# Loads, weight conversions, merges and the last stores rearranged in a Fourier mixing and gated feed-forward kernel

## The chip, the cores and the metric

The kernel runs on one core of one Trainium2 chip. The time is device time of one execution in microseconds (us); several executions are taken, and their median counts. Engines: PE does the matmuls (PEld its weight loads), DVE and POOL work elementwise on SBUF, ACT evaluates functions and copies, SP only issues transfers. DVE and ACT also read PSUM, where matmuls write. Every engine runs its own instructions in program order; semaphores order the engines among each other.

## The reference

Two stages with one tensor between them. The shapes are batch 8, sequence 3008, width 256, hidden width 1536.

```python
X = np.fft.fft(x, axis=1)
X = np.fft.fft(X, axis=2)
x = X.real.astype(np.float32).reshape(8 * 3008, 256)
gate = 1.0 / (1.0 + np.exp(-(x @ w_gate)))
val = x @ w_val
out = (gate * val @ w_out).astype(np.float32)
```

x is float32. The three weight matrices arrive as float64 and are read as pairs of 32-bit words.

## The kernel before

**Mixing.** The real part of a 2-D transform is a cosine sum minus a sine sum. Rows s, S-s, M+s and M-s of the sequence are loaded together (`x4`, 126 partitions x 4 x 6 x 256), and `fold_ops` adds and subtracts them: `point` (L222) adds a row to its mirror, `first` (L225) does column 0, the unnamed pair at L237 and L238 adds and subtracts the two halves, and `feat` (L228 to L230) folds the features. The sums over the sequence are matmuls with a cosine and a sine table `st` (`half`, groups of an even and an odd PSUM bank, `ev` and `od`); ACT copies `ev` to `a` (L276), and DVE adds and subtracts it with `od` (`places`, L280 and L283) into `pk` (cosine), `qk` (sine) and `ek` (the middle feature). The transform over features isn't done on the data: it is merged into the weights, `merge` (L188) multiplies the table `dt` with a block of gate or value weights, and ACT copies the result to `G1` and `G2`; two small transfers then bring one row of `G2` to `ge` (L198).

**Feed-forward.** For each batch, 6 chunks of sequence positions (five of 256, the last 225) and 6 pairs of hidden blocks, two steps per pair. A step is: `front`, four products `pa` and `pb` on PE and `ae`, `z`, `z` on DVE (L343, L346, L347); `gate` of the step before, `h` on DVE (L358) and one or three sums `sf` on POOL; `back` of the pair two before, 3 or 4 products into the PSUM banks `po0` to `po3`; then the sigmoid on ACT (L543), one entry of the list `later` and the entries of `side`. After a chunk's last pair `finish` copies the banks to `c7` (ACT, L399), adds the slots (POOL, on DVE for the last chunk), transposes 32x32 blocks into `os` (DVE, L406) and stores them with SP, four transfers for each of two halves of the output rows, and four more for rows beyond the last full block of 32.

**Weights.** There are 18 jobs: gate, value and output blocks in turn (0 and 1: gate and value of block 0; 2, 3, 4: gate and value of block 1, output of block 0; and so on). A job is: a load of 512 KB on SP; `weight_parts`, two instructions of ACT; `weight_join`, three of DVE (L174, L175, L177) and one add of POOL (L179), which together turn float64 into float32; then `weight_use`, that is `merge` for gate and value, and `forms` for the output weights (two copies on ACT, four subtractions on POOL). The raw words of jobs 0 to 4 lie in the three places of the tile `z`; those of later jobs lie in `mega`, which takes the space of batch 0's `x4`, and a job's load there waits for the add of the job three before.

**Order.** It is written out by hand and nothing is rearranged. In the opening, loads are issued (x and cosine table in thirds, weights 0 and 1, sine table in thirds, weights 2 to 4); three folds and the cosine products follow, then conversions 0 and 1 between the evacuations, the sine products with merges 0 and 1 between them (L467 to L471), conversions 2 to 4 and the sines' evacuation. Within a step, `pre` is run before the sigmoid (conversions of later weights on ACT), `side` after it (their joins, the loads three jobs ahead, and the uses). Block c of the weights is first needed in step 2c.

```python
    for i in range(2 * len(pairs)):
        done, fresh = fresh, front(i // 2, i % 2)
        if done is not None:
            gate(*done)
        if i >= 4:
            back(i // 2 - 2, i % 2)
        for f in pre.pop(i, []):
            f()
        z = fresh[2]
        nc.scalar.activation(z[:, 0], z[:, 0], AF.Sigmoid)
        if later:
            later.pop(0)()
        for f in side.pop(i, []):
            f()
```

PSUM banks of the opening and of `pa`, `pb` and the merges come from one ring of four (`psx`).

Of the kernel before, what the change touches and what calls it, by code (L numbers as in the profile page):

```python
# [45 lines left out]
def kernel(  # L46
# [56 lines left out]
    def rows(out, src):  # L103

        m = NP // 16 * 16
        nc.sync.dma_start(out=out[0:m], in_=src[0:m])
        nc.sync.dma_start(out=out[m:NP], in_=src[m:NP])

    def load_x(b, nq):
        X[b] = xp.tile([NP, 4, NQ, D], F32, name="x4", tag="x4")  # L110
        return [lambda q=q: rows(X[b][:, :, q : q + nq], xf[b, :, :, q : q + nq])
                for q in range(0, NQ, nq)]
# [11 lines left out]
    def load_table(t, nq):  # L124
        return [lambda q=q: rows(st[:, t, q : q + nq], stab[:, t, q : q + nq])
                for q in range(0, NQ, nq)]
# [7 lines left out]
    KEEP = 5  # L134

    def weight_load(j):

        w, c = jobs[j]
        src = (moe_w_gate, moe_w_val, moe_w_out)[w]
        src = src[2 * c * P : 2 * (c + 1) * P, :] if w == 2 else src[:, c * WC : (c + 1) * WC]  # L140
        src = src.rearrange("(c p) f -> p c f", p=P)
        if j < KEEP:
            raw = zp.tile([P, 2, WC, 2], I32, name="raw", tag="z")
            ws = (app if j < 3 else hp).tile([P, 2, WC], F32, name="ws", tag="ae" if j < 3 else "h")
        else:
            if not mega:
                mega.append(xp.tile([P, 12, 2 * WC], F32, name="mega", tag="x4"))
            r, i = (j - KEEP) % 3 * 2, 6 + (j - KEEP) % 6
            raw = mega[0][:, r : r + 2].rearrange("p a n -> p (a n)").bitcast(I32).rearrange(
                "p (c f w) -> p c f w", c=2, w=2)  # L150
            ws = mega[0][:, i].rearrange("p (c f) -> p c f", c=2)
        WS[j] = ws
        if src.dtype == F32:
            nc.sync.dma_start(out=ws, in_=src)
        else:
            RAW[j] = raw
            nc.sync.dma_start(out=raw.rearrange("p c f w -> p c (f w)"), in_=src.bitcast(I32))
# [58 lines left out]
    def fold_ops(b, eng, nq):  # L216
        x4 = X.pop(b)
        tt = eng.tensor_tensor
        ops = []

        def point(i, j, q):
            tt(x4[:, i, q, 1:D], x4[:, i, q, 1:D], x4[:, j, q, D - 1 : 0 : -1], op=ALU.add)  # L222

        def first(i, j, q):
            tt(x4[:, i, q, 0], x4[:, i, q, 0], x4[:, j, q, 0], op=ALU.add)  # L225

        def feat(v, r, q):
            eng.memset(r[:, q, 0:1], 0.0)  # L228
            tt(r[:, q, 1:HD], v[:, q, 1:HD], v[:, q, D - 1 : HD : -1], op=ALU.subtract)  # L229
            tt(v[:, q, 1:HD], v[:, q, 1:HD], v[:, q, D - 1 : HD : -1], op=ALU.add)  # L230

        parts = [(x4[:, 1 + 2 * blk], x4[:, 2 * blk]) for blk in range(2)]
        qs = [slice(q, q + nq) for q in range(0, NQ, nq)]

        def kind(q):
            two = [[lambda i=i: point(i, i + 1, q)] for i in (0, 2)]
            return two + [[lambda: tt(x4[:, 1, q], x4[:, 0, q], x4[:, 2, q], op=ALU.add)],  # L237
                          [lambda: tt(x4[:, 3, q], x4[:, 0, q], x4[:, 2, q], op=ALU.subtract)]] + [  # L238
                [lambda v=v, r=r: feat(v, r, q)] for v, r in parts]

        if b:

            for n, group in enumerate(zip(*[kind(q) for q in qs])):
                ops += [f for fs in group for f in fs]
                if n < 2:
                    ops.append(lambda n=n: first(2 * n, 2 * n + 1, slice(0, NQ)))
        else:

            for q in qs:
                part = []  # L250
                for n, fs in enumerate(kind(q)):
                    part += fs
                    if n < 2:
                        part.append(lambda n=n, q=q: first(2 * n, 2 * n + 1, q))
                ops.append(lambda part=part: [f() for f in part])
        for blk, (v, r) in enumerate(parts):
            W[b, blk] = (v[:, :, 0:HD], r[:, :, 0:HD],
                         v[:, :, HD : HD + 1].to_broadcast([NP, NQ, P]))
        return ops
# [113 lines left out]
    def back(p, part):  # L373
        b, c, i = pairs[p]
        n = chunks[c][1]
        if part == 0 and i == 0:
            PO[:] = [pso.tile([P, 2, CH], F32, name=f"po{t}", tag=f"po{t}") for t in range(4)]
        h, s = H[p], SF[p]
        move = {1: h[:, 0, 0], 2: h[:, 1, 0], 3: s[:, 3], 4: h[:, 1, 1], 5: s[:, 0], 6: s[:, 1],
                7: s[:, 2]}  # L380
        for m in ORDER[part]:
            t, j = SLOT[m]
            mm(PO[t][:, j, 0:n], wf[:, i, m - 1], move[m], i == 0 and m in FIRST,
               i == NPR - 1)
        if part == 0 and i == NPR - 1:
            PO.append(cp.tile([P, 7, CH], F32, name="c7", tag="c7"))
            nc.scalar.copy(PO[4][:, 6, 0:n], PO[3][:, 0, 0:n])
        if part:
            del H[p], SF[p]
            if i == NPR - 1:  # L390
                finish(b, c, nc.vector if p == len(pairs) - 1 else nc.gpsimd)

    def finish(b, c, eng):
        k0, n = chunks[c]
        nb = -(-n // TB)
        t = PO[4]
        os_ = op.tile([P, 2, CH // TB, 2, TB], F32, name="os", tag="os")
        for j in (0, 2, 1):
            nc.scalar.copy(t[:, 2 * j : 2 * j + 2, 0:n], PO[j][:, :, 0:n])  # L399
# [3 lines left out]
        tt = eng.tensor_tensor  # L403
# [4 lines left out]
        def store(s):  # L408
# [3 lines left out]
            full = m // TB  # L412
            for a in range(4):
                ps = slice(a * TB, (a + 1) * TB)
                cs = slice(a * 2 * TB, (a + 1) * 2 * TB)
                nc.sync.dma_start(
# [6 lines left out]

        later.extend([
# [23 lines left out]
    for j in range(2, KEEP):  # L448
        weight_load(j)
    seq_start(0)  # L450
    folds0 = fold_ops(0, nc.vector, 2)
    cos = [seq_group(0, blk, what, (2 * blk, 2 * blk + 1) if what else None)
           for what in (0, 2) for blk in range(2)]
    for i, f in enumerate(folds0):
# [7 lines left out]
    cos[1][1]()()  # L462
    weight_join(1)
    for _, then in cos[2:]:
        then()()
# [6 lines left out]
    for j in range(2, KEEP):  # L472
        weight_parts(j)
    for _, then in sin:
        then()()
    for j in range(2, KEEP):
        weight_join(j)
# [13 lines left out]
    def weight_step(i, *js):  # L491

        for j in js:
            pre.setdefault(i, []).append(lambda j=j: weight_parts(j))
            at(i, lambda j=j: weight_join(j))
            if j + 3 < len(jobs):
# [3 lines left out]
    for c in range(1, NPR):  # L500
        i = 2 * (c - 1)
        j = 3 * c - 1
        at(i, lambda j=j: weight_use(j))
        at(i + 1, lambda j=j: weight_use(j + 1))
        at(i + (c > 1), lambda j=j: weight_use(j + 2))
        if c + 1 < NPR:
            weight_step(i, j + 3)
            weight_step(i + 1, j + 4, j + 5)
        else:
            weight_step(i, j + 3)  # L510
            at(i + 1, lambda j=j: weight_use(j + 3))
# [3 lines left out]
    for b in range(B - 1):  # L515
# [5 lines left out]
        def folds(f0=f0, b=b):  # L521
            for j, f in enumerate(fold_ops(b + 1, nc.gpsimd, 2)):
# [83 lines left out]
```

## Time and profile before

| | |
|---|---|
| Median of 9 runs | 2045.38 us (2044.51 to 2048.5) |
| Profiled execution | 2045.07 us, span of its records 2043.1 us |
| PE busy | 2003.1 us (98%), 9168 matmul passes |
| DVE busy | 1752.0 us (86%), 3239 instructions |
| POOL busy | 1323.5 us (65%) |
| ACT busy | 500.4 us (24%) |
| Granted TensorE clock, mean | 0.993 |
| HBM traffic | 44.50 MB read, 24.68 MB written |

Parts of the span, from the timeline: loads, folds and the first sums up to about 44 us; the first `pa` at 47.4 us; conversions and merges of weights beside steps 0 to 9, up to about 113 us; after that PE without a pause until its last pass ends at 2033.4 us; sums, transposes and stores of the last chunk until 2043.1 us. The chain of waits that ended last lies on PE for 84% of the span, on DVE for 8% and on POOL for 4%.

How to read the lines: the page gives busy tenths in 40 slices of the span (some 51 us each), with the clock that was granted to PE in tenths. A timeline line has start, duration, engine, source line, operation, tile written <- tiles read, shape, how many instructions were merged into the line, and in brackets the idle time before it with what ended it. Lines of the windows give start:end, length, busy time and number of instructions of each engine, the granted clock, the busy share of the DMA engines, and GB/s. A line of waits gives who waited for whom, the sum, how often, and the longest. "SPq" and "ACTq" are the issues of transfers on those engines' queues.

### The profile page before, as it was taken

What the parts mean: (1) busy time and instruction counts of PE and PEld (TensorE: products, weight loads), DVE (VectorE), ACT (ScalarE), POOL (GpSimd) and SP (SyncE); (2) the same over time, 40 slices, a digit from 0 to 9 for tenths busy, and PEclk for the clock granted to TensorE, in tenths of its full rate; (3) what the DMA queues carried; (4) which work ended last, traced back from release to release, by engine and by line L of the source; (5) the groups of instructions that cost most, each with busy time, mean ns of one, the idle gap of its engine ahead of it and who ended that gap; (6) DMA issues with size and microseconds to landing.
All of it is one profiled execution on the core that took longest, in us unless ns stands there. A gap on an engine that the chain in (4) does not pass through costs nothing.

```text
span 2043.1 us, 27431 instructions
## 1 busy us (share of the span) xinstructions
PE 2003.1 (98%) x9168; PEld 1743.0 (85%) x9168; DVE 1752.0 (86%) x3239; ACT 500.4 (24%) x878; POOL 1323.5 (65%) x1669
## 2 busy tenths in 40 slices
PE   6799999999999999999999999999999999999998
PEld 3688789888898889988898888988889888898887
DVE  4989778988799878998789978899778988898887
ACT  2522222222222222222222222222222222222222
POOL 0768645885569755697457955589446875565654
PEclk9899999999999999999999999999999999999999
DMA  9351003010031000300012000301003010000001
GB/s 238 103 64 21 27 11 72 15 31 11 11 77 31 11 11 11 81 26 12 11 30 62 26 15 18 72 10 33 15 11 72 15 31 11 11 16 16 11 16 25
DMA packets 143530, 70.98 MB, mean 35 GB/s; under 512 B 128299, under 2 KB 128555, under 8 KB 143390
## 3 DMA queue, kind: packets, MB, share of 16 engines
q1 hardware_dynamic: 142528, 68.93, 14.8%
q8 instruction: 74, 1.21, 0.3%
q14 instruction: 66, 0.54, 0.1%
q10 hardware_dynamic: 862, 0.31, 0.1%
HBM read 44.50 MB, written 24.68 MB: 34 GB/s over the span
## 4 chain that ended last, share of the span: by engine, by line
PE 84%; DVE 8%; POOL 4%; DMA 2%; issue 1%; ACT 0%; SPq 0%; DVEq 0%; ACTq 0%; POOLq 0%
PE po L93 37%; PE pa L93 21%; PE pb L93 21%; PE ev L93 3%; PE od L93 3%; DVE ae L343 2%; DVE h L358 2%; DVE z L347 1%; DMA st<-in_stab_dram 1%; DVE z L346 1%; POOL x L230 1%; POOL x L229 1%; POOL sf L363 1%; POOL sf L362 1%; DVE os L406 0%
## 5 line engine op out<-in xcount | busy, mean ns | idle before, releaser
L543 ACT ACTIVATE z<-z 128x512 f32<-128x512 f32 (+1 forms) x576 | 358.6, 623 | 1309.8 <-DVE z L347 1309.8
L343 DVE SCALAR_TENSOR_TENSOR ae<-ek,ge,pa 128x256 f32<-128x256 f32 (+1 forms) x1152 | 490.0, 466 | 191.6 <-PE pa L93 187.8
L93 PE MATMUL pa<-pk,G 128*128 128x256 f32 (+1 forms) x2304 | 585.3, 376 | 13.4 <-ACT G L196 9.9
L93 PE MATMUL pb<-qk,G 128*128 128x256 f32 (+1 forms) x2304 | 584.0, 376 | 0.0
L93 PE MATMUL po<-sf,wf 128*128 128x256 f32 (+1 forms) x2304 | 537.1, 375 | 0.8
L93 PEld LDWEIGHTS pa<-pk,G 128*128 128x128 f32 x2304 | 438.3, 191 | 73.4 <-ACT G L196 12.3
L93 PEld LDWEIGHTS po<-sf,wf 128*128 128x128 f32 x2304 | 436.2, 190 | 55.6 <-POOL sf L364 4.5
L93 PEld LDWEIGHTS pb<-qk,G 128*128 128x128 f32 x2304 | 439.5, 191 | 50.4
L362 POOL TENSOR_TENSOR sf<-h 128x256 f32<-128x256 f32 (+1 forms) x288 | 213.1, 740 | 395.8 <-DVE h L358 395.8
L358 DVE TENSOR_TENSOR h<-z 128x512 f32<-128x512 f32 (+1 forms) x576 | 448.8, 779 | 0.0
L346 DVE TENSOR_TENSOR z<-ae,pb 128x512 f32<-128x512 f32 (+1 forms) x576 | 390.1, 677 | 61.4 <-DVE ae L343 1.8
L93 PE MATMUL po<-h,wf 128*128 128x256 f32 (+1 forms) x1728 | 413.1, 375 | 0.0
L347 DVE TENSOR_TENSOR z<-ae,pb 128x512 f32<-128x512 f32 (+1 forms) x576 | 386.0, 670 | 0.0
L93 PEld LDWEIGHTS po<-h,wf 128*128 128x128 f32 x1728 | 328.9, 190 | 37.4
L360 POOL TENSOR_TENSOR sf<-h 128x256 f32<-128x256 f32 (+1 forms) x288 | 218.8, 760 | 210.2 <-DVE h L358 206.9
L364 POOL TENSOR_TENSOR sf<-h,sf 128x256 f32<-128x256 f32 (+1 forms) x288 | 214.9, 746 | 22.6
L363 POOL TENSOR_TENSOR sf<-sf,h 128x256 f32<-128x256 f32 (+1 forms) x288 | 214.6, 745 | 22.6
L399 ACT COPY c<-po 128x512 f32<-128x512 f32 (+1 forms) x144 | 78.5, 580 | 64.7 <-PE po L93 64.6
L93 PE MATMUL ev<-st,x 126*128 126x377 f32 (+3 forms) x216 | 77.9, 487 | 14.9 <-DVE x L230 14.0
L406 DVE STREAM_TRANSPOSE os<-c 128x256 f32<-128x256 f32 x192 | 83.5, 436 | 0.0
L93 PE MATMUL od<-st,x 126*128 126x377 f32 (+3 forms) x216 | 76.8, 482 | 0.0
L428 POOL TENSOR_TENSOR c<-c 128x512 f32<-128x512 f32 (+1 forms) x47 | 74.1, 1576 | 0.0
(72 smaller groups left out, 709.9 us busy)
## 6 DMA issues: line engine op xcount, KB each, us to landing
x<-in_xf_dram SPq DMA_DIRECT2D x14, 1344.0 KB
out_dram<-os SPq DMA_DIRECT2D x288, 64.0 KB
out_dram<-os SPq DMA_DIRECT2D x96, 56.0 KB
ek<-ed SPq DMA_DIRECT2D x7, 752.5 KB
st<-in_stab_dram SPq DMA_DIRECT2D x6, 658.9 KB
x<-in_xf_dram SPq DMA_DIRECT2D x3, 896.0 KB
mega<-in_moe_w_out_dram SPq DMA_DIRECT2D x5, 512.0 KB
x<-in_xf_dram SPq DMA_DIRECT2D x14, 168.0 KB
```

The lines of the kernel that those rows point to most:

```text
L93: nc.tensor.matmul(o, l, r, start=start, stop=stop, skip_group_check=True)
L343: nc.vector.scalar_tensor_tensor(out=ae[:, g], in0=ek[:, ks], scalar=ge[:, g, f : f + 1], in1=pa[:, g], op0=ALU.mult, op1=ALU.add)
L346: nc.vector.tensor_tensor(z[:, :, 0], ae, pb, op=ALU.add)
L347: nc.vector.tensor_tensor(z[:, :, 1, ::-1], ae, pb, op=ALU.subtract)
L358: nc.vector.tensor_tensor(h[:, fh], z[:, 0], z[:, 1], op=ALU.mult)
L360: tt(s[:, 2], h[:, 0, 0], h[:, 0, 1], op=ALU.subtract)
L362: tt(s[:, 0], h[:, 0, 1], h[:, 1, 1], op=ALU.add)
L363: tt(s[:, 1], s[:, 0], h[:, 0, 0], op=ALU.subtract)
L364: tt(s[:, 3], h[:, 1, 0], s[:, 1], op=ALU.subtract)
L399: nc.scalar.copy(t[:, 2 * j : 2 * j + 2, 0:n], PO[j][:, :, 0:n])
L406: nc.vector.transpose(os_[:, s, 0:nb, h, :], t[:, slot, 0 : nb * TB])
L543: nc.scalar.activation(z[:, 0], z[:, 0], AF.Sigmoid)
```

## The change

Five things are changed. (1) `rows`, which cut each load of x and table into 112 and 14 rows, is gone: 126 rows go in one transfer. (2) Raw words of jobs 3 to 7 get places of their own (second copies of `pk`, `qk`, `ek`, and the two places of `c7`), so eight jobs are loaded in the opening before `x4` is free, and jobs 8 to 10 are the first in `mega`. (3) `fold_ops`: for batch 0, the first third is folded by DVE as before, in another order; of the other two, DVE folds one half (`point` of rows 0 and 1, sum, features) and POOL the other. The cosine groups are ordered by block. (4) In the opening, conversions 2 and 3 with their joins stand ahead of the sines' evacuation and 4 behind it; in the steps, each weight's use comes one step earlier, while its conversion stays where it was. (5) The last chunk's sums read the PSUM banks directly, without ACT's copies except that of `po3`, in another order, with the transposes between them; its stores alternate between SP's and ACT's queues, and in every batch's last chunk the single row beyond the last full block goes out in one transfer instead of four.

```diff
-    def rows(out, src):
-
-        m = NP // 16 * 16
-        nc.sync.dma_start(out=out[0:m], in_=src[0:m])
-        nc.sync.dma_start(out=out[m:NP], in_=src[m:NP])
...
-        return [lambda q=q: rows(X[b][:, :, q : q + nq], xf[b, :, :, q : q + nq])
+        return [lambda q=q: nc.sync.dma_start(out=X[b][:, :, q : q + nq], in_=xf[b, :, :, q : q + nq])
...
-    KEEP = 5
+    KEEP = 8
...
-        if j < KEEP:
-            raw = zp.tile([P, 2, WC, 2], I32, name="raw", tag="z")
+        if j < 6:
+            if j < 3:
+                raw = zp.tile([P, 2, WC, 2], I32, name="raw", tag="z")
+            else:
+                raw = pqp.tile([P, 2, WC, 2], I32, name="raw", tag=("pk", "qk", "ek")[j - 3])
             ws = (app if j < 3 else hp).tile([P, 2, WC], F32, name="ws", tag="ae" if j < 3 else "h")
         else:
+            if j < KEEP:
+                both = cp.tile([P, 3, 2 * WC], F32, name="both", tag="c7")
+                r, i = 0, 2
...
+            def part(q, es):
+                for e, i in zip(es, (0, 2)):
+                    point(e, i, i + 1, q)
+                    first(e, i, i + 1, q)
+                across(es[0], 0, q)
+                feat(es[0], *parts[0], q)
+                across(es[1], 1, q)
+                feat(es[1], *parts[1], q)
+            for n, q in enumerate(qs):
+                ops.append(lambda q=q, es=(nc.vector, pool if n else nc.vector): part(q, es))
...
+        queues = (nc.sync, nc.scalar) if last else (nc.sync,)
...
+            if m - full * TB == 1:
+                nc.sync.dma_start(
+                    out=out[r0 + m - 1 : r0 + m].rearrange("o (a d) -> (o a) d", d=2 * TB),
+                    in_=os_[0:P:TB, s, full].rearrange("p h j -> p (h j)"))
+                m -= 1
             for a in range(4):
...
-                nc.sync.dma_start(
+                queues[a % len(queues)].dma_start(
...
+        if last:
+
+            o = [q[:, :, 0:n] for q in PO[0:3]]
+            tt(v[:, 0:2], v[:, 6:7].to_broadcast([P, 2, n]), o[0], op=ALU.add)
+            flip(0, 0, 0)
+            tt(v[:, 3], v[:, 1], o[1][:, 1], op=ALU.add)
+            tt(v[:, 5], v[:, 3], o[2][:, 1], op=ALU.add)
+            flip(1, 0, 5)
+            tt(v[:, 1], v[:, 1], o[1][:, 0], op=ALU.add)
+            tt(v[:, 4], v[:, 1], o[2][:, 0], op=ALU.add)
+            flip(0, 1, 4)
+            store(0)
+            tt(v[:, 2], v[:, 3], o[1][:, 0], op=ALU.add)
+            flip(1, 1, 2)
+            store(1)
+            return
...
     cos = [seq_group(0, blk, what, (2 * blk, 2 * blk + 1) if what else None)
-           for what in (0, 2) for blk in range(2)]
+           for blk in range(2) for what in (0, 2)]
...
-    for j in range(2, KEEP):
+    for j in range(2, 4):
         weight_parts(j)
+        weight_join(j)
     for _, then in sin:
         then()()
-    for j in range(2, KEEP):
-        weight_join(j)
+    weight_parts(4)
+    weight_join(4)
...
-            if j + 3 < len(jobs):
+            if KEEP <= j < len(jobs) - 3:
                 at(i, lambda j=j: weight_load(j + 3))
...
+    for c in range(1, NPR + 1):
+        i, j = 2 * c - 3, 3 * c - 1
+        if c < NPR:
+            at(max(i, 0), lambda j=j: weight_use(j))
+            at(i + 1, lambda j=j: weight_use(j + 1))
+            at(i + 2, lambda j=j: weight_use(j + 2))
+        else:
+            at(i, lambda j=j: weight_use(j))
+        if c == NPR:
+            weight_step(i - 1, j)
+        elif c > 1:
+            weight_step(i - 1, j)
+            weight_step(i, j + 1, j + 2)
```

In the old order the uses of block c's gate, value and the output block before it stood in steps 2c-2, 2c-1 and 2c-1 (2c-2 for c = 1); in the new one they stand in steps 2c-3, 2c-2 and 2c-1 (both merges of block 1 in step 0).

## The prediction

> **What bounds it now.** I read the page's slices first, then the windows of the first 120 us, the waits, the timeline there, and the timeline of the last 20 us. The slices:
>
> ```profile
> PE   6799999999999999999999999999999999999998
> DVE  4989778988799878998789978899778988898887
> PEclk9899999999999999999999999999999999999999
> DMA  9351003010031000300012000301003010000001
> ```
>
> From the third slice on PE is full at full clock: 30 matmul passes per pair in 6.47 us, DVE about 86% beside it. The diff changes no work there, so nothing is to be won or lost between about 118 and 2027 us. What can move is the first 118 us and the tail. By stage (us; busy of PE, PEld, DVE, ACT, POOL; granted clock; DMA share; GB/s):
>
> ```profile
> 28.00:32.00 4.00, 3.61 (x12) 1.86 (x10) 3.34 (x8) 2.55 (x6) 0.74 (x1) 1.00 1.04 259
> ...
> 44.00:48.00 4.00, 0.64 (x2) 0.55 (x3) 0.66 (x2) 3.75 (x9) 0.00 (x0) 0.83 0.73 230
> 48.00:52.00 4.00, 3.14 (x8) 1.93 (x6) 3.90 (x8) 1.18 (x2) 1.08 (x1) 0.50 0.43 163
> ...
> 70.00:80.00 10.00, 8.87 (x40) 7.44 (x39) 9.61 (x16) 5.99 (x13) 8.76 (x10) 0.97 0.33 101
> 80.00:90.00 10.00, 7.24 (x34) 6.06 (x33) 9.70 (x16) 5.21 (x12) 8.13 (x10) 1.00 0.55 157
> ```
>
> Three stages: up to 43 us the loads (DMA share 1.0); 44 to 47 ACT, which converts weights 2 to 4 while PE idles and drops to half clock; from 47 to 111 DVE at 96%, with its own step work (ae, z, z, h: 2.9 us) plus 1.5 joins per step. PE's waits there:
>
> ```profile
> PE pa L93 <- ACT G L196: 9.9, 6, 3.1
> PE pa L93 <- ACT a L276: 3.5, 1, 3.5
> ```
>
> The 9.9 us look like the prize and mostly are not: DVE is full meanwhile. A PE wait counts only where PE is afterwards continuous to the end, and that is from step 8's second pa at 100.93 us:
>
> ```profile
> 100.93 0.97 PE L93 MATMUL pa<-pk,G 128*128 128x256 f32 x2 [2.12 <-ACT G L196]
> 103.60 1.74 POOL L179 TENSOR_TENSOR mega<-mega 128x512 int32<-128x512 int32 x1
> ```
>
> **The parts.** All against the profiled execution (2045.07 us, span 2043.1, about 2 us around it); the median of the nine runs is 0.3 higher. No change can be told from a change of under 0.2%, 4.1 us.
>
> *Unsplit loads.* Twelve issues become six; x, the tables and dt with weights 0 and 1 up to the sine table's first third are 7.44 MB (issue sizes of the page), and its second piece, 14 rows, issued at 18.09, landed at 32.48, where PE waited. SP's issues were held by waits for earlier loads (25 us in sum); half as many issues relax that. How fast 126 rows in one piece go, the trace doesn't show. Ends: 410 GB/s, the best 1.5 us slice (weights, 128 rows): 7.44/0.41 = 18 us, so 13 us earlier, of which folds and cosines let some 8 through; 168 GB/s, the worst slice: 44 us, 13 late. Nearest is the same data in two pieces: about 255 GB/s, 29.2 us from 1.5 on, 1.8 earlier than measured. I take no gain, 32.5: **0 (-8 to +13)**, and every us of lateness lands one for one on what follows.
>
> The Trainium skill speaks against this part: "DMA: Bandwidth & Descriptors", section "Why a DMA increments its semaphore by 16 and not by 1", says a transfer uses the largest number of engines up to 16 that divides its row count, so 126 rows get 14 and the old 112 got 16. By it alone the 6.13 MB of x and table would take an eighth longer, an estimate of 3.0 us late. The trace has no view that shows engines per transfer; the 255 against 410 GB/s says that something besides engine count already holds the split loads back.
>
> *First folds.* Parts 1 and 2 give the second block (point, first, across, two feats) to POOL. DVE rows: 0.69 + 0.16 + 0.69 + 0.06 + 0.42 + 0.42 = 2.4 us for one block; the POOL rows of the later folds: 1.42 + 0.43 + 1.27 + 0.10 + 0.87 + 0.84 = 4.9. Side by side both are done 4.9 us after x lands, one after the other 7.4; now 4.5 on DVE alone. Halfway: 6.2, first block 4.4. From x's third landing at 22.55: PE has block 0 at 27.0, block 1 at 28.7, and with its 16 passes of 0.317 us ends the cosines at 32.0. The sines wait for the table until 32.5 anyway: **cost 0**. At the serial end evacuation holds a PSUM bank of the sines some 1.2 us: 0 to +1.2.
>
> Here the skill takes the serial side: "SBUF — State Buffer", section "SBUF: two separate sides", says GpSimd and a VectorE operation with two SBUF inputs exclude each other for a whole instruction. The trace agrees at the end of the run, where h took 1.02 us beside a POOL operation and 0.62 alone.
>
> *Places and order of conversions.* Eight places: weights 5 to 7 no longer wait for x's space (issued at 43.9). Their conversions stand where they stood, so that hides. What moves: conversions 2 and 3 stay ahead of the sines' copies on ACT, 4 goes behind, and joins 2 and 3 go ahead of the sines' sums on DVE. ACT is free at 43.58 (behind two ge issues of 1.76 us). Two conversions at 1.09 us each: the copies begin at 45.8, before 46.85. DVE: join 2 from 44.24, 1.6 us; join 3 2.4 us (its L175 takes 1.38 beside POOL's add); four sums of 0.46: 50.05, where they ended at 49.2. Join 4 1.5 us: step 0's ae could start at 51.5 instead of 55.66. But now step 0 carries two merges, both ahead of step 1's pa in PE's queue. PE at half clock until about 55.5: pb0 50.1 to 52.0 (1.91 in its row), merge 2 to 55.7 (its row: 3.78), merge 3 at full clock 1.73, pa1 0.86: ae of step 1 at 58.4, which was 59.79. So of 4.2 us DVE gets **-1.4**; with no half clock the merges would take 2 us less (-3.4), with all four at half clock 2.6 more (+1.2).
>
> *Merges one step ahead.* (a) Step 6's ae waited 0.76 for ge: gone, **-0.8**. (b) PE was last held at 100.93 and at half clock until 103.3, and ended job 14's merge at 107.04; then job 15's merge, steps 9 and on, with 0.3 lost at 113. In the new order job 15's merge comes at the end of step 8, behind POOL's add for it (L179, 103.60 + 1.74 = 105.34 less the 2.2 us of shift), with the same work left. 107.04 - 105.34 + 0.3 = **-2.0**. The new wait: each merge now stands in PE's queue right behind POOL's add of the step before, and the next pa, which ae needs, behind the merge. Cover, step by step: job 9's add ended at 80.0, merge 1.73 + pa 0.86 gives 82.6, ae came at 84.36; job 11: 88.9 against 91.25; job 12: 94.8 against 97.22; job 14: 101.7 against 104.1. So 1.7 to 2.4 us of cover, at full clock; without it DVE stalls in each of eight steps. With one more half-clock window of 3.4 us: +1.7.
>
> *Tail.* The last chunk's lines:
>
> ```profile
> 2033.36 0.54 ACT L399 COPY c<-po 128x450 f32<-128x450 f32 x1 [0.22 <-PE po L93]
> 2035.63 1.42 DVE L406 STREAM_TRANSPOSE os<-c 128x256 f32<-128x256 f32 x4
> 2036.43 2.31 SPq L416 DMA_DIRECT2D out_dram<-os  x5
> 2040.90 0.30 SPq L420 DMA_DIRECT2D out_dram<-os  x1
> ```
>
> After PE's last pass (2033.3): sums of 225 columns take 0.40 from SBUF, and ae, which reads PSUM, 0.44 at that width, so 0.42 each; transposes 0.36. Three sums, a sum of two and four transposes in the new order reach store 0 at 2035.9 (was 2036.4) and store 1 at 2036.65. Then SP issued twelve transfers one by one until 2041.2. Now SP has five (0.46, 0.46, 0.34, 0.36, 0.36): 2037.9; ACT has four, at 0.44 to 0.88 by its own issue rows: 2037.9 to 2039.4. So 1.8 to 3.3 earlier, in the middle 2.5, less some 0.5 for transfers that now overlap: **-2.0 (-1 to -3.3)**. The merged single-row stores of the other batches leave SP, which waits for transposes for most of the span: 0.
>
> Sum: 0 + 0 - 1.4 - 0.8 - 2.0 - 2.0 = -6.2: 2038.9 profiled, **2039.2** for the median.
>
> **Rivals.**
>
> *Unsplit tables come late* (slower side). Place: the sines' first matmul, now held to 32.58. Each us costs one; at 6.2 late (7.44 MB in 37.2 us: 200 GB/s) nothing is gained, and from 10.3 late, 180 GB/s, the run is measurably slower. At the worst slice's 168: 2045.4 + 13.3 - 6.2 = **2052.5**. For it: slices of 168 to 205 occur while split pieces mix. Against: they last 1.5 us, between stretches of 250 to 300. A milder case, 219 GB/s (the slices of 211 and 228 late in this stage), is 3.0 late and leaves **2042.2**.
>
> *They come early.* At rates between the ends the sines start up to 8 us earlier, half of which I count: **2035**. For it: fewer issues, waits of SP gone, no 14-row stragglers.
>
> *PE starved behind the adds.* Half clock eats the cover. Two steps need 9.9 us of PE and last 12.95; if a share s of 60 to 105 us is at half clock, PE needs 9.9(1+s), beyond the cover from s = 0.31. With four such pairs, the 4.2 us won in this stage are gone at s = 0.31 + 4.2/39.6 = 0.42, mean clock 0.79: **2043.4**. Against: the clock there is now 0.92 or so, and PE's gaps become shorter and more even.
>
> *The moved order doesn't act*: the merges' queue gives back the same 4.2 us even at full clock, and only the tail remains: **2043.4**.
>
> **Chances.** Forecast (2036.3 to 2041.9: half clock 2.0 down or 1.7 up, the tail 1 each way) 0.45; early 0.17; late but mild 0.13, late to slower 0.12; starved or not acting 0.13. Faster by over 0.2% (below 2041.3): nearly all of the forecast, the early case and a third of the mild lateness, 0.65; slower: 0.12; within: 0.23. The 8 in 10 take in early loads to 2032 and lateness to 2046.
>
> **What would show it.** The sines' first matmul later than 33 us: loads; earlier than 31: they gained. SP's first eight loads issued before 8 us. PE's waits for G gone from the list, waits of ps for POOL in their place, each under 2.5 us. Step 1's ae near 58.4; PE continuous from about 103. The last stores issued about 5 us after PE's last pass instead of 8, from both queues. I would be wrong in kind if ae waited for pa in every early step, or if the granted clock stayed near half past 60 us.

## The result and the profile after

The changed kernel takes 2037.25 us in the median of 9 runs (2035.05 to 2042.84); the kernel before took 2045.87 us in the median of the 29 runs made beside it. The ratio is 0.9958 with a 95% interval of 0.9950 to 0.9966, so it is 8.6 us faster; the prediction said 6.2. The profiled execution is one of the longer ones: 2042.48 us, span 2040.7, only 2.6 below the profiled execution of before. What the nine runs gained and this one did not is the first thing to explain.

The busy tenths of the changed kernel, in 40 slices of the span:

```profile
PE   6799999999999999999999999999999999999998
...
DVE  4999778988799878998789988899878988798887
PEclk9899999999999999999999999999999999999999
DMA  8241102010021000200012000201002010000001
```

From the third slice on PE's row and the clock's are unchanged, as expected. The difference lies in the first 120 us and the last 10. The windows of the changed kernel there (us; busy of PE, PEld, DVE, ACT, POOL; granted clock; DMA share; GB/s):

```profile
28.00:32.00 4.00, 3.35 (x11) 2.08 (x12) 0.75 (x2) 1.58 (x3) 1.83 (x4) 1.00 1.00 228
32.00:36.00 4.00, 1.99 (x8) 0.91 (x6) 3.82 (x9) 2.38 (x5) 1.29 (x1) 1.00 0.95 238
36.00:40.00 4.00, 4.00 (x8) 2.27 (x9) 2.76 (x6) 0.07 (x1) 1.29 (x1) 0.63 0.94 283
...
44.00:48.00 4.00, 4.00 (x17) 2.90 (x16) 0.00 (x0) 0.65 (x2) 0.00 (x0) 1.00 0.24 74
48.00:52.00 4.00, 2.09 (x8) 0.91 (x6) 3.14 (x5) 3.96 (x8) 1.36 (x1) 1.00 0.50 128
...
70.00:80.00 10.00, 10.00 (x37) 8.22 (x37) 8.49 (x14) 5.78 (x13) 6.84 (x8) 0.77 0.20 53
```

The work runs some 3.4 us later than in the first windows of before. The stage in which ACT converts weights (44 to 48 before, 48 to 52 now) no longer leaves DVE idle: 3.14 us busy of 4, where it had 0.66. The half clock behind the 0.77 of 70 to 80 us lies from about 67.5 to 74.5 us. The kernel before had the like from 63.5 to 70.5, so it has moved with the loads:

```profile
60.00:70.00 10.00, 6.43 (x16) 4.84 (x16) 9.60 (x17) 6.16 (x14) 4.78 (x5) 0.68 0.38 110
```

New is the half clock from about 37 to 40.5 us (0.63 over 36 to 40), inside the sines. PE's waits from 28 to 118 us:

```profile
PE ps L93 <- POOL mega L181: 6.0, 5, 2.5
PE ps L93 <- POOL both L181: 4.0, 1, 4.0
PE pb L93 <- DVE qk L287: 2.4, 1, 2.4
PE ev L93 <- DMA st<-in_stab_dram: 2.0, 1, 2.0
PE pa L93 <- ACT a L283: 1.8, 1, 1.8
...
```

The waits of `pa` for `G` (9.9 us before) are gone, and waits of the merges, `ps`, for POOL's adds stand in their place (10.0 us). The sines' first matmul waited for the table until 35.98 us, where it had been 32.58. Yet PE reaches steady work at the same place: step 12's first `pa` starts at 119.25 us in this execution and at 119.27 in that of before. So 3.4 us lost on the loads were won back between the sines and step 12, and 2.6 us were won at the end. The last chunk's lines of the changed kernel:

```profile
2031.44 1.90 PE L93 MATMUL po<-sf,wf 128*128 128x225 f32 x8
...
2032.10 0.62 DVE L438 TENSOR_TENSOR c<-c,po 128x450 f32<-128x450 f32 x1 [2.44 <-PE po L93]
...
2035.89 1.89 ACTq L427 DMA_DIRECT2D out_dram<-os  x4
...
2036.79 0.56 SPq L420 DMA_DIRECT2D out_dram<-os  x1
2037.39 0.92 SPq L427 DMA_DIRECT2D out_dram<-os  x2
```

PE's last pass ends at 2033.34 as before, and the last issue 5.0 us behind it (7.9 before); the span ends 7.4 us behind it (9.8 before).

### The profile page after: what moved, and what is told of

The parts are those of the page before. It is cut to its first block, busy times and chain, and to the rows that moved or that the text cites. A ratio compares the mean times of both kernels' runs of the same rounds, so it can differ in the third digit from the quotient of the medians.

```text
span 2040.7 us, 27360 instructions
## 1 busy us (share of the span) xinstructions
PE 2000.0 (98%) x9168; PEld 1740.6 (85%) x9168; DVE 1751.8 (86%) x3228; ACT 498.9 (24%) x875; POOL 1334.5 (65%) x1681
## 4 chain that ended last, share of the span: by engine, by line
PE 85%; DVE 7%; POOL 4%; DMA 1%; issue 1%; SPq 1%; ACT 0%; DVEq 0%; ACTq 0%; POOLq 0%
PE po L93 37%; PE pa L93 21%; PE pb L93 21%; PE ev L93 3%; PE od L93 3%; DVE ae L350 2%; DVE h L365 2%; DVE z L354 1%; DMA st<-in_stab_dram 1%; POOL x L233 1%; DVE z L353 1%; POOL x L231 1%; PE ps L93 1%; POOL sf L370 1%; POOL sf L369 1%
## 5 line engine op out<-in xcount | busy, mean ns | idle before, releaser
L93 PEld LDWEIGHTS pa<-pk,G 128*128 128x128 f32 x2304 | 438.0, 190 | 59.5 <-ACT a L283 2.4
L452 ACT COPY c<-po 128x512 f32<-128x512 f32 (+1 forms) x141 | 76.9, 581 | 64.0 <-PE po L93 64.0
L93 PEld LDWEIGHTS ev<-st,x 126*128 126x128 f32 (+1 forms) x216 | 40.0, 188 | 42.0 <-DVE x L233 17.6
```

Of the source, the lines that this page charges most:

```text
L93: nc.tensor.matmul(o, l, r, start=start, stop=stop, skip_group_check=True)
```

## How the runs are compared

A time of one execution falls into three parts that the profile dates: the start of the sines' first matmul (S; loads, folds and cosines before it), the stretch from S to step 12's first `pa` (T), behind which PE never stops, and the rest of the time. Each row below is one profiled execution beside the median of the timed runs of that kernel. "to ae 1" is the part of the stretch up to `ae` of step 1; all us. A ratio is taken against runs of the kernel before that were made beside the row's own.

| kernel | S | to ae 1 | stretch S to T | rest | median (range, runs) | ratio to before |
|---|---|---|---|---|---|---|
| before | 32.6 | 27.2 | 86.7 | 1925.8 | 2045.87 (2044.51 to 2048.5, 29) | |
| after | 36.0 | 25.4 | 83.3 | 1923.2 | 2037.25 (2035.05 to 2042.84, 9) | 0.9958 [0.9950, 0.9966] |
| again | 34.6 | 23.9 | 81.9 | 1923.5 | 2037.72 (2036.36 to 2041.27, 5) | 0.9959 [0.9947, 0.9971] |
| split_loads | 32.7 | 24.0 | 81.9 | 1923.2 | 2040.3 (2037.75 to 2040.79, 5) | 0.9964 [0.9952, 0.9976] |
| merges_late | 29.4 | 22.8 | 81.4 | 1923.5 | 2037.2 (2034.3 to 2040.41, 5) | 0.9952 [0.9940, 0.9964] |
| dve_folds | 37.0 | 23.8 | 81.7 | 1924.4 | 2040.24 (2035.94 to 2045.9, 11) | 0.9968 [0.9957, 0.9980] |
| first_merge_late | 30.6 | 22.8 | 80.3 | 1923.8 | 2034.68 (2033.29 to 2039.89, 5) | 0.9951 [0.9938, 0.9964] |
| early_conversions | 33.0 | 23.7 | 81.7 | 1923.8 | 2040.02 (2033.65 to 2043.49, 6) | 0.9965 [0.9952, 0.9978] |
| old_tail | 29.7 | 24.6 | 82.6 | 1926.0 | 2044.51 (2038.24 to 2047.23, 11) | 0.9985 [0.9975, 0.9995] |
| unsplit_alone | 32.5 | 26.6 | 86.1 | 1926.5 | 2045.69 (2042.01 to 2052.74, 11) | 1.0002 [0.9993, 1.0012] |
| order_undone | 39.4 | 28.3 | 87.7 | 1923.2 | 2041.34 (2038.72 to 2050.55, 11) | 0.9983 [0.9971, 0.9994] |
| combined | 30.6 | 19.9 | 76.9 | 1923.7 | 2035.8 (2029.42 to 2036.74, 5) | 0.9940 [0.9927, 0.9953] |
| combined_split | 32.9 | 20.2 | 76.8 | 1923.2 | 2033.15 (2032.82 to 2034.79, 5) | 0.9938 [0.9926, 0.9951] |
| combined_table_first | 35.5 | 22.0 | 79.1 | 1924.3 | 2035.86 (2034.29 to 2038.94, 5) | 0.9949 [0.9935, 0.9963] |

How to read it: the stretch answers for the order of the work, and the rest for the tail. Five of these profiles (after, again, split_loads, dve_folds, old_tail) have the same order behind S; their stretches lie within 81.7 to 83.3, and the rest is 1923.2 and 1923.5 in the two profiles of the changed kernel. S differs by 10 us between the profiles, and it is S that makes one profile look better than another. A median is therefore worth more than one profile where the loads are concerned, and a stretch is worth more than a median where the order is. The profiled execution of after is 1.4 us behind the second profile of the same kernel, again (83.3 against 81.9). All of that arises up to step 1's `ae` (25.4 against 23.9): the half clock inside the sines is in the one and not in the other. The same two passes in after, then in again:

```profile
37.60 1.46 PE L93 MATMUL ev<-st,x 126*128 126x376 f32 x2
```

```profile
35.91 0.79 PE L93 MATMUL ev<-st,x 126*128 126x376 f32 x2
```

The sines' first third with the merge behind it took 6.0 us (35.98 to 42.01) against 4.3 (34.56 to 38.90).

Half clock is not what separates the kernels before and after. Between 36 and 118 us before spent 20.5 us at half clock, after and again 13.7 each, but unsplit_alone, which has the order of before, only 10.2, and its stretch is still 86.1. In combined 3.4 us are left, and no run separates how much of its gain comes from that.

## The experiments

**again**: the changed kernel without an edit, run beside split_loads, merges_late and dve_folds.

> The changed kernel unaltered, for a second profile beside its times: the profiled execution of the change took 2042.48 us, 5 us more than the median of its nine runs, and in it the sines' first matmul waited for the table until 35.98 us. Theory (the unsplit loads arrive at a time that varies, early in most executions): an execution near 2037 starts its sines at 30 to 32 us and enters step 12 near 114. Rival (the spread comes from later, from the granted clock or the waits of merges for POOL): sines again near 36 us whatever the time, and step 12 is entered early all the same.

Measured: 2037.72 us, S at 34.6, stretch 81.9. The sines started late again, so lateness is no accident of the first profile; but with the rest and the stretch of this row, the nine times of after (mostly 2035 to 2038) put S between some 30 and 33 us in most executions (2037.25 - 1923.5 - 81.9 = 31.9): worked out, not seen.

**split_loads**: the old row split in the changed kernel.

```diff
+    def rows(out, src):
+        m = NP // 16 * 16
+        nc.sync.dma_start(out=out[0:m], in_=src[0:m])
+        nc.sync.dma_start(out=out[m:NP], in_=src[m:NP])
...
-        return [lambda q=q: nc.sync.dma_start(out=X[b][:, :, q : q + nq], in_=xf[b, :, :, q : q + nq])
+        return [lambda q=q: rows(X[b][:, :, q : q + nq], xf[b, :, :, q : q + nq])
...
-        return [lambda q=q: nc.sync.dma_start(out=st[:, t, q : q + nq], in_=stab[:, t, q : q + nq])
+        return [lambda q=q: rows(st[:, t, q : q + nq], stab[:, t, q : q + nq])
```

> The changed kernel with x and tables loaded in 112 and 14 rows again. Theory (unsplit loads are worth some 4 to 5 us): 2041 to 2043, sines near 33 us. Rival (the loads gain nothing, the order of conversions and merges does): 2036 to 2038.

Measured: 2040.3 us, interval of the ratio 0.9952 to 0.9976 against 0.9950 to 0.9966 of the changed kernel: no difference that can be told, and a median between the theory's and the rival's. S at 32.7, where the kernel before has it, though in this run PE waited for a copy of ACT (0.34 us) and not for the table.

**unsplit_alone**: the reverse, the kernel before with loads of 126 rows and nothing else.

```diff
-        m = NP // 16 * 16
-        nc.sync.dma_start(out=out[0:m], in_=src[0:m])
-        nc.sync.dma_start(out=out[m:NP], in_=src[m:NP])
+        nc.sync.dma_start(out=out, in_=src)
```

> The kernel before with only the loads of x and tables in one piece. Theory (what loads do is start the sines sooner or later; by times less the fixed rest, sines start at 29.6 to 37.4 us in the changed kernel, 32 to 36 before): a median 1 to 2 us below before, with executions from 2042 to 2049. Rival (the page's rule, 14 of 16 engines): 3 us slower, 2049, in every execution.

Measured: ratio 1.0002, interval 0.9993 to 1.0012. In the median no worth of the unsplit loads can be told, and nothing is the value that the prediction took. What they do is spread the times: 11 runs over 10.7 us, where the 29 of the kernel before lie within 4.0.

**dve_folds**: all of batch 0's folds on DVE.

```diff
-                ops.append(lambda q=q, es=(nc.vector, pool if n else nc.vector): part(q, es))
+                ops.append(lambda q=q, es=(nc.vector, nc.vector): part(q, es))
```

> The changed kernel with batch 0 folded by DVE alone. In the changed kernel's profile the last third took 5.9 us to fold (24.04 to 29.97) against 4.5 before, and the sines then waited for the table. Theory (hidden behind the table's load): 2036.5 to 2038, no difference. Rival (in a typical execution the table is there early and the folds bind): 1 to 1.5 us faster, 2035.5 to 2036.5.

Measured: 2040.24 us, ratio 0.9957 to 0.9980; not to be told from the changed kernel, and outside the ranges of theory and rival. The timelines show what the shared folds do. The last third in the changed kernel, DVE and then POOL:

```profile
24.04 0.69 DVE L223 TENSOR_TENSOR x<-x 126x510 f32<-126x510 f32 x1 [2.08 <-DMA x<-in_xf_dram]
24.65 1.23 DVE L227 TENSOR_TENSOR x<-x 126x2 f32<-126x2 f32 x1
26.04 0.69 DVE L236 TENSOR_TENSOR x<-x 126x512 f32<-126x512 f32 x1 [0.17 <-POOL x L227]
...
27.22 1.37 DVE L233 TENSOR_TENSOR x<-x 126x254 f32<-126x254 f32 x1
```

```profile
24.08 1.77 POOL L223 TENSOR_TENSOR x<-x 126x510 f32<-126x510 f32 x1 [0.74 <-DMA x<-in_xf_dram]
...
28.43 0.74 POOL L231 TENSOR_TENSOR x<-x 126x254 f32<-126x254 f32 x1
29.25 0.72 POOL L233 TENSOR_TENSOR x<-x 126x254 f32<-126x254 f32 x1
```

And the same instructions on DVE alone, in dve_folds:

```profile
25.49 0.15 DVE L227 TENSOR_TENSOR x<-x 126x2 f32<-126x2 f32 x1
...
29.06 0.42 DVE L233 TENSOR_TENSOR x<-x 126x254 f32<-126x254 f32 x1
```

The sum of column 0 takes 1.23 us beside POOL and 0.15 alone, the feature fold 1.37 and 0.42: DVE stands still inside the instruction until POOL's has ended. From the landing of x the shared folds take 5.9 us (24.04 to 29.97), DVE alone 4.6 (24.88 to 29.48). The longer fold is hidden as long as the table is later still. Where x and table come early it can bind: in merges_late the cosines' last third waited 0.65 us for a fold on DVE, and the sines followed at 29.4 us without a wait for a load.

**merges_late**: all uses of weights in the steps where they were before, the rest as changed.

```diff
-    for c in range(1, NPR + 1):
-        i, j = 2 * c - 3, 3 * c - 1
-        if c < NPR:
-            at(max(i, 0), lambda j=j: weight_use(j))
-            at(i + 1, lambda j=j: weight_use(j + 1))
-            at(i + 2, lambda j=j: weight_use(j + 2))
+    for c in range(1, NPR):
+        i = 2 * (c - 1)
+        j = 3 * c - 1
+        at(i, lambda j=j: weight_use(j))
+        at(i + 1, lambda j=j: weight_use(j + 1))
+        at(i + (c > 1), lambda j=j: weight_use(j + 2))
...
```

> The changed kernel with every weight's use in the step where it was. Theory (each merge moved ahead saves what was predicted, 2.0 + 0.8 us, and step 0 is relieved of its second merge, worth up to 1.4 the other way): 2038 to 2040, PE's waits for G back at some 8 to 10 us. Rival (PE now waits for POOL's adds as long as it did for G): 2036 to 2038, no difference.

Measured: 2037.2 us and a stretch of 81.4, against 2037.25 to 2037.72 and 81.9. PE's waits in merges_late look as bad as in the kernel before, and the stretch is 5 us shorter all the same:

```profile
PE pa L93 <- ACT G L198: 9.2, 5, 3.9
PE pa L93 <- ACT a L283: 2.1, 1, 2.1
...
```

So merges one step ahead earn nothing in sum that can be told. The two parts of the stretch say why: step 1's `ae` is reached 1.1 us sooner without them (22.8 against 23.9, since step 0 has one merge instead of two), and the part behind it is 0.7 longer (58.6 against 57.9).

**first_merge_late**: the merges stay one step ahead, except that of block 1's value weights, which goes back to step 1.

```diff
-            at(i + 1, lambda j=j: weight_use(j + 1))
+            at(i + 1 + (c == 1), lambda j=j: weight_use(j + 1))
```

> The changed kernel with one merge (val of block 1) back in step 1, so that step 0 has one merge and not two; all later merges stay one step ahead. Moving all merges back had cost nothing: 81.4 us from the sines' first matmul to step 12's pa, 81.9 with them ahead, 86.7 before the change. Theory (moving ahead earns 2.8 us in steps 5 to 10 and loses as much in step 0, where step 1's pa stands behind two merges): 79 to 80 us from sines to step 12, ae of step 1 some 2.5 us earlier after the sines, median about 2035. Rival (the moved merges earn nothing in the later steps): 81.5 us again, 2037.

Measured: stretch 80.3, with 22.8 up to step 1's `ae` and 57.5 behind it: the better part of both. By stretch it is 1.6 us better than the changed kernel; the ratio, 0.9938 to 0.9964, cannot tell it from that.

**early_conversions**: conversions 2 to 4 with their joins ahead of merges 0 and 1 in the opening.

```diff
+        if i == 0:
+            for j in range(2, 5):
+                weight_parts(j)
+                weight_join(j)
         if i < 2:
             weight_use(i, i)
-    for j in range(2, 4):
-        weight_parts(j)
-        weight_join(j)
     for _, then in sin:
         then()()
-    weight_parts(4)
-    weight_join(4)
```

> The changed kernel with conversions 2, 3 and 4 on ACT and their joins on DVE ahead of merge 0's copies, in the 8 to 10 us in which DVE now waits after the cosines; the sines' evacuation directly follows the sines. Theory (DVE's work after the sines is what the steps wait for, and three joins of 1.6 to 2.4 us leave it): 76 to 78 us from sines to step 12, 2032 to 2034. Rival (PE's two merges in step 0 hold step 1 whatever DVE does): 80 to 81 us, 2036 to 2037.

Measured: stretch 81.7, 2040.02 us: nothing won. DVE's waits show what took the place of the conversions:

```profile
DVE ws L176 <- ACT ws L166: 4.3, 1, 4.3
DVE ae L350 <- PE pa L93: 3.2, 2, 1.7
...
DVE ae L350 <- DMA ge<-G: 1.6, 1, 1.6
...
```

The merges of the opening and with them `ge` came later, and PE carried two merges ahead of step 1's `pa`, so `ae` waited 4.8 us for PE and `ge`. So drawing the conversions alone further ahead won nothing here: what they freed, PE held.

**order_undone**: merges, conversions, joins and the sines' evacuation in the old order; places, loads, folds and tail as changed.

```diff
-    for j in range(2, 4):
+    for j in range(2, 5):
         weight_parts(j)
-        weight_join(j)
     for _, then in sin:
         then()()
-    weight_parts(4)
-    weight_join(4)
+    for j in range(2, 5):
+        weight_join(j)
...
```

The uses of weights are put back by the same lines as in merges_late.

> The changed kernel with the merges' steps and the order of conversions, joins and the sines' evacuation as before; the eight places, the unsplit loads, the shared folds and the new tail stay. Read from the trace: us from the sines' first matmul to step 12's first pa (86.7 in the kernel before, 83.3 and 81.9 in two profiles of the changed one, 81.4 with only the merges put back). Theory 1, the order of conversions earns the 5 us: the stretch is 85 to 87 again, step 0's ae starts about 23 us behind the sines' first matmul, and the median is 2041 to 2042. Rival, the eight places earn it (weights 5 to 7 are there earlier): the stretch stays at 81 to 82 and the median at 2037 to 2038.

Measured: stretch 87.7 and 2041.34 us; some 1.7 us of the stretch is half clock inside the sines, as in after (their first third with its merge takes 6.0 us here too). The whole gain of the stretch is gone, so the eight places for raw words earn nothing by themselves. Since merges_late takes back the merges alone and keeps the gain, the order of conversions earns it. Whether that order needs the eight places is open: no run has it with five. The window in which ACT converts, in order_undone:

```profile
52.00:56.00 4.00, 1.12 (x6) 0.68 (x4) 0.81 (x2) 4.00 (x9) 0.00 (x0) 1.00 0.61 191
```

ACT is full, DVE has 0.81 us of work in 4 and PE 1.12: the stage of the kernel before, back again. The joins stand behind the evacuation on DVE, and the evacuation's copies behind three conversions on ACT.

**old_tail**: the last chunk's copies, sums and stores as before.

```diff
-        queues = (nc.sync, nc.scalar) if last else (nc.sync,)
+        queues = (nc.sync,)
...
-            if m - full * TB == 1:
...
-                m -= 1
...
-        if last:
...
-            return
```

> The changed kernel with the last chunk copied by ACT, summed from SBUF and stored by SP alone, single rows in four transfers, as before the change. Theory (the tail is worth its share of the profile, 2.4 us from PE's last pass to the end): 9.7 us from PE's last pass to the end of the span where the change has 7.3; median 2039 to 2040. Rival (the stores' landing and not their issue ends the run): under 1 us of difference.

Measured: the rest is 1926.0 us, against 1923.2 and 1923.5 with the new tail. Its last pass ends at 2026.66 in a span of 2036.4: 9.7 us, as before, against 7.4. The median is 7 us above that of the changed kernel, of which the tail explains 2.5; its eleven runs fall into two groups (2038.2 to 2039.3 and 2043.5 to 2047.2), and the unsplit loads, which spread other kernels as far, are the likely reason. This run does not show it.

**combined**: what the runs had suggested, put together. Folds on DVE; the table's thirds and weights 0 to 2 taken in turns by SP; the cosines evacuated ahead of three conversions, these ahead of the sines' sums; merges 0 and 1 and conversion 3 behind the second third of the sines; conversion 4 behind their evacuation; block 1's value merge in step 1; every `ge` transfer on SP.

```diff
...
-    weight_parts(0)
-    cos[0][1]()()
-    weight_parts(1)
-    weight_join(0)
-    cos[1][1]()()
-    cos[2][1]()()
-    weight_join(1)
-    cos[3][1]()()
+    for g in (0, 2, 1, 3):
+        cos[g][1]()()
+    for j in range(3):
+        weight_parts(j)
+        weight_join(j)
...
-        if i < 2:
-            weight_use(i, i)
-    for j in range(2, 4):
-        weight_parts(j)
-        weight_join(j)
+        if i == 1:
+            weight_use(0, 0)
+            weight_use(1, 1)
+            weight_parts(3)
+            weight_join(3)
...
-            at(i + 1, lambda j=j: weight_use(j + 1))
+            at(i + 1 + (c == 1), lambda j=j: weight_use(j + 1))
```

> The changed kernel with what the runs so far suggest put together: batch 0's folds on DVE alone, the table's thirds between weights 0, 1 and 2 in SP's queue, three conversions ahead of the sines' sums on ACT (the cosines' evacuations first), merges 0 and 1 behind the second third of the sines, conversion 4 behind their evacuation, the val merge of chunk 1 in step 1 and the other merges one step ahead. Theory 1, DVE's and ACT's order bound this stage: the stretch from the sines' first matmul to step 12's first pa is 76 to 78 us (81.9 in the changed kernel, 80.3 with the one merge moved), the sines start at 29.5 to 31, and the median is 2030 to 2033. Rival, PE's merges and the two sine groups hold it whatever the order of conversions: the stretch stays at 80, the sines start near 32, and the median is 2034.5 to 2036.

Measured: stretch 76.9 and S 30.6, both as the first theory had them; the five times spread from 2029.42 to 2036.74 and their median, 2035.8, is that of the rival. The order of the work held. That the loads spoilt the median is likely and not shown: by the rest and the stretch of this row, 2036.74 us would put S at 36.1.

**combined_split** and **combined_table_first**: combined with the row split of before, and combined with all weights behind the sine table in SP's queue.

```diff
-    for n, f in enumerate(load_table(1, 2)):
+    for f in load_table(1, 2):
         f()
-        if n < 2:
-            weight_load(n)
-    for j in range(2, KEEP):
+    for j in range(KEEP):
         weight_load(j)
```

> The combined kernel (2035.8 us median, 2029.42 to 2036.74) with x and the tables loaded in 112 and 14 rows again. So far the kernels with 126 rows in one piece spread over 4 to 12 us (unsplit_alone 2042.0 to 2052.7, old_tail 2038.2 to 2047.2, order_undone 2038.7 to 2050.6) and their profiles have the sines' first matmul anywhere from 29.4 to 39.4 us; the two profiles with split loads have it at 32.6 and 32.7, and the spreads are 3 to 4 us. Theory 1, the one-piece loads make the spread: the five times lie within 3.5 us, the sines' first matmul is at 31.5 to 33.5 us, and the median is 2032 to 2034.5. Rival, the spread comes from the order of the work behind the loads (half-clock windows that fall differently): the times lie over 6 us or more again and the median is 2035 to 2037.

> The combined kernel with all weights behind the sine table in SP's queue, so that the loads up to there are all of 126 rows and of one form. Theory 1, the spread comes from loads of 128 rows beside those of 126: the times lie within 4 us, the sines' first matmul is at 27 to 30 us, the stretch from there to step 12's first pa grows to 78 to 81, since the weights land later, and the median is 2031 to 2034. Rival, the one-piece loads vary by themselves: the times lie over 6 us or more, the last third of x is folded anywhere between 24 and 30 us as before, and the median is 2034 to 2038.

Measured: with split loads the five times lie within 2.0 us (2032.82 to 2034.79), S is at 32.9 and the stretch at 76.8. This is the best median of the study: 12.7 us below the 2045.87 us of the kernel before (13.2 below the nine runs of it made beside these), 4.1 below the changed kernel, all five runs below the fastest of its nine. Five runs carry this, and its interval (0.9926 to 0.9951) just touches that of the changed kernel. With all weights behind the table S did not come sooner but later (35.5), and the first theory of that run fell: loads of 126 rows can be late without any loads of 128 rows but `dt` beside them. Its five times spread over 4.7 us, between the 4 of the theory and the 6 of the rival, so the spread's cause stays open. The windows from 3 to 6 us and 18 to 21 us, first in the kernel before, then in combined_table_first:

```profile
3.00:6.00 3.00, 0.00 (x0) 0.00 (x0) 0.00 (x0) 0.00 (x0) 0.00 (x0) 1.00 1.06 308
18.00:21.00 3.00, 3.00 (x11) 1.66 (x10) 1.61 (x6) 0.00 (x0) 0.00 (x0) 1.00 1.15 268
```

```profile
3.00:6.00 3.00, 0.00 (x0) 0.00 (x0) 0.00 (x0) 0.00 (x0) 0.00 (x0) 1.00 0.82 275
18.00:21.00 3.00, 3.00 (x10) 1.67 (x9) 2.86 (x9) 0.00 (x0) 0.00 (x0) 1.00 1.07 232
```

In the first window the share of the DMA engines' time is 0.82 with loads of 126 rows (0.88 in the changed kernel) and 1.06 with split ones, at 275 (293) and 308 GB/s. Over all profiles the share is the steady difference, 0.82 to 0.89 in the eleven with 126 rows and 1.05 to 1.06 in the three with split loads; the rate is not (275 to 317 against 301 to 321 GB/s). From 18 to 21 us the one-piece loads ran at anything from 232 to 331 GB/s, the split ones at 263 to 268: they are uneven, not always slower.

## Why the prediction was right, point by point

*Unsplit loads, 0 (-8 to +13).* Right in the median (unsplit_alone, 1.0002), and the breadth of the range was earned: S lay anywhere from 29.4 to 39.4 us in the profiles with loads of 126 rows, and from 32.6 to 32.9 in the three with split ones. Two of the rivals, tables that come early and tables that come a little late, both happened, in kernels whose loads and folds are the same (S at 29.4 in merges_late, 36.0 in after); that is what the prediction's single value hid. The reason it gave for an earlier start, fewer issues held up on SP, did not act: SP's third table issue took 4.4 us and weight 0 was issued at 10.2 us, so the named sign "eight issues before 8 us" failed. Why the 126-row loads vary is open.

In the first window the DMA share was 0.82 to 0.89 with 126 rows. The Trainium skill, "DMA: Bandwidth & Descriptors", section "Why a DMA increments its semaphore by 16 and not by 1", gives 126 rows 14 engines and 112 rows 16. The share fits 14 of 16 engines (0.875). The prediction's estimate from that rule, an eighth longer or 3.0 us, should have been a seventh (16 to 14) and some 3.4. The median shows no such loss: unsplit_alone lies within -1.4 and +2.5 us of the kernel before by its interval.

*First folds, 0 (0 to +1.2).* The working took the middle between side by side and one after the other, 6.2 us with the first block done after 4.4; measured were 5.9 and 4.6 us. It cost nothing that a median could show.

The Trainium skill, "SBUF — State Buffer", section "SBUF: two separate sides", had said that one of the two engines waits for a whole instruction of the other. The 1.37 us against 0.42 and the 1.23 against 0.15 agree with it.

*Places and order of conversions, -1.4 to step 1's `ae`.* Measured -1.8 in the profile (25.4 against 27.2), -3.3 in again, split_loads and dve_folds (23.8 to 24.0), and -2.6 in old_tail (24.6). The gross gain of the order, which the working put at 4.2, is 4.4 (merges_late, 22.8, which has one merge in step 0). What was mis-sized is the second merge in step 0: 2.8 us in the working, with PE at half clock in it, 1.1 in the runs. That the order and not the places alone earns it is shown by order_undone and merges_late together.

*Merges one step ahead, -0.8 and -2.0.* This is the term that was too large. Behind step 1's `ae` the stretch shrank by 1.5 us (57.8 to 57.9 in the five profiles of this order, 59.5 before), and merges_late has 0.9 of that too. So the merges' places earn some 0.7, not 2.8. The smaller part, step 6's wait for `ge`, did go as forecast: DVE's waits from 28 to 118 us in after name no `ge`. The place where PE was last held moved as forecast in kind but not in size; the timeline of the changed kernel:

```profile
105.70 2.98 POOL L181 TENSOR_TENSOR mega<-mega 128x512 int32<-128x512 int32 x2
...
107.49 1.99 PE L93 MATMUL ps<-mega,dt 128*128 128x256 f32 x8 [1.19 <-POOL mega L181]
...
109.32 1.03 PE L93 MATMUL pa<-pk,G 128*128 128x256 f32 x4
```

Job 15's merge still waited 1.19 us for POOL's add, so PE runs without a pause from 107.49, or 71.5 us after the sines' first matmul; the kernel before had the same work left at 107.04, 74.5 us after its own. The waits for POOL were each 2.5 us or less but for one of 4.0. The sign "continuous from about 103" missed here, by the 3.4 us of late loads and about one more, for which the half clock in the sines is enough. In again that merge starts at 104.68, 70.1 us after the sines; with the sines at the working's 32.5 that is 102.6.

*Tail, -2.0 (-1 to -3.3).* Measured 2.4 (9.8 to 7.4 us behind PE's last pass), and 2.5 by old_tail. The last issue 5.0 us behind PE's last pass is the sign that was named.

*The sum.* By the stretches, -4.8 (81.9 against 86.7) stands against the -4.2 of the three order terms, and -2.4 against -2.0. These make 7.2 of the 8.6 us, and that they come so near is in part luck: the order of conversions was forecast 1.9 us too small (-1.4 against -3.3), the merges 1.3 too large (-2.8 against the -1.5 behind step 1's `ae`), and the two misses nearly cancel. As for the rest, 1.4 us would be S, earlier in most executions than the 32.6 of the profile before. That is a difference of sums, not seen in a profile. The profiled execution adds up: +3.4 loads, -3.4 stretch, -2.6 rest: 2045.07 - 2.6 = 2042.5.

The rival "starved behind the adds" had its waits (10.0 us of PE behind POOL's adds) but not its clock: from 60 to 105 us the mean was 0.92 in after and again, and the rival began to cost below 0.85 (a share of 0.31). In the kernel before it was 0.89 there, not the 0.92 that the prediction read. "The moved order doesn't act" holds for one half of it: for the merges, not for the conversions.

## What to carry to other kernels

A wait list names the engine that is late, not what the lateness costs: 9.9 us of PE's waits went away and another 10.0 came, and the gain came from a stage that PE's list hardly named (3.5 us for a copy of ACT), one in which DVE had nothing to do behind ACT. Date the execution at two or three fixed events and compare the stretches between them; a part that varies from run to run (here the loads) then no longer hides a steady gain of 5 us. And judge a load by its spread as well as by its median.

## What the runs showed that was not expected

- Loads of 126 rows in one piece leave a median alone and widen the spread: 10.7 against 4.0 us in the kernel before, 7.8 against 3.0 in the changed one, 7.3 against 2.0 in combined. Three pairs agree, though the second five runs of the changed kernel, again, spread over only 4.9; the cause is not found.
- Issuing a transfer can hold SP for long: 4.39 us for the third load of the cosine table, where the five before it took 0.53 to 1.50.
- Putting one merge back by one step shortens the stretch by 1.6 us (81.9 to 80.3), more than moving all the others ahead does (81.4 to 80.3); one profile each, where profiles of one order differ by up to 1.6.
